# Retention and a softplus feed-forward layer on one core: step 8's scores moved behind step 7's values, and the weights loaded and converted in another order

## The chip, the cores and the metric

The kernel runs on one core of one Trainium2 chip. The metric is the device time of one execution in microseconds (us); the kernel before has a median of 818.29 us over three runs (818.12 to 818.95). A core has five engines with a queue each, which run their own instructions in program order: TensorE (PE, with its weight loads as PEld), VectorE (DVE), ScalarE (ACT), GpSimd (POOL) and SyncE (SP, which issues the DMA transfers here). They wait for each other through semaphores.

## The reference

```python
def _attn_ref(q, k, v):                      # batch 8, heads 8, sequence 576, head width 64
    scores = scale * np.matmul(q, k.transpose(0, 1, 3, 2))
    Dmat = np.where(rel >= 0, gamma[:, None, None] ** rel[None, :, :], 0.0)
    return np.matmul(scores * Dmat[None, :, :, :], v)
def _moe_ref(x, w_in, w_out):                # 4608 tokens, 512 -> 2048 -> 512
    h = x @ w_in
    g = np.maximum(h, 0.0) + np.log1p(np.exp(-np.abs(h)))
    return g @ w_out
```

The attention output, with its heads side by side, is the `x` of the feed-forward layer.

## The kernel before

The attention is computed in its recurrent form, in **steps** of two head pairs by 128 tokens. For each step TensorE makes scores (`scores`, `scores_whole`), sums of keys and values (`sums`), values (`values`), and the products with the state so far ("cross"). VectorE masks the scores into `a` (or `a_whole`), updates the state `s`, and scales the values out into `x`. ScalarE scales the step's `v` in place (`scale_values`; for steps 9 and later GpSimd does it), and writes the high part of `x` into `xt`; the low part (`x` minus the high part) is a subtraction on GpSimd or VectorE. The feed-forward products run as three products of high and low parts.

The 4608 tokens are nine units of 512. The **opening** (`for m in range(AHEAD)`, AHEAD = 9, FIRST = 8) does steps 0 to 7 for unit 0 whole, and begins step 8 for unit 1. Then come 16 **slots** (`for i in range(NF)`): slot i makes `h` for hidden block i of unit 0 (12 matmuls, from first-layer weight `win i`), its softplus, and the 12 output matmuls `y` of the block before (from second-layer weight `wout i-1`). Every odd slot also has the next attention step in front of its `h`. After the slots the tail of the kernel begins with one more attention product group (`chunk_products` of steps 17 and 16), followed by products whose weights come through a ring of buffers (`ring`).

**Weights.** There are 32 weight pieces of 512 KB, piece 2p for `win p` and 2p+1 for `wout p`. They lie in memory in 64 bits, and each is converted while it is used for the first time: `weight_p` (ScalarE, high word), `weight_t` (VectorE, low word), `weight_b` (VectorE, joins them in `wst`), `weight_c` (ScalarE, high part into `win` or `wout`), `weight_d` (VectorE, low part). They stage through the five buffers of `wst`; `weight_dl` does the last part, starts the load of a further piece into a freed buffer, and stores a first-layer piece back to memory in its two parts (`split`). The function `weight_a` is `weight_p` and `weight_t`.

The order on each engine is the order in which the code is written. All loads go through SP's queue: eight semaphores are used in turn, so that a load waits until the load eight places ahead of it has landed, and a wait holds back whatever stands behind it.

When the last weight is through, the pool of `wst` is closed, and its memory goes to the ring and to the buffers named `odd`, one of which takes the `qv` (queries and values) of step 17:

```python
if n + 2 >= NPIECE and "ring" not in later:
    weight_pools.close()
    ...
    load_step(2 * CHUNKS - 1)
    scale_values(2 * CHUNKS - 1)
    for _ in range(RING):
        block_load()
```

Of the kernel before, what the change touches and what calls it, by code (L numbers as in the profile page):

```python
# [27 lines left out]
NF = DF // P  # L28
# [9 lines left out]
NCONST = SMALL + NPAIR * C  # L38
PIECE = 512
FIRST = AHEAD - 1  # L40
START_WEIGHTS = 3
OPENING = 3
NOPEN = AHEAD + 2
CHUNKS = 9
# [39 lines left out]
def retention_softplus_ffn(ctx: ExitStack, tc, first, whole, others, consts, w, out):  # L84
# [73 lines left out]
    def load_step(m):  # L158

        if m == 0:  # L160
            at = 0
            for x in parts:
                nc.sync.dma_start(x, first[:, at:at + x.shape[1]])
                at += x.shape[1]
            k, q = parts[0][:, 0:2 * C], parts[0][:, 2 * C:4 * C]
            kp, v = parts[1][:, 0:2 * C], parts[1][:, 2 * C:4 * C]
        else:
            if m < NOPEN:
                place = openp if m < OPEN1 else openp2
                r = place.tile([P, 8 * C if m < FIRST else RAW], F32, name=f"raw{m}")  # L170
                nc.sync.dma_start(r, whole[m - 1] if m < FIRST else others[m - FIRST])
                keys, qv = r[:, 0:KEYS], r[:, KEYS:]
            else:
                load_keys(m)
                load_rest(m)
                return
            k, kp, q, v = keys[:, 0:2 * C], keys[:, 2 * C:], qv[:, 0:-2 * C], qv[:, -2 * C:]
        live[m] = {n: x.rearrange("p (s c) -> p s c", s=2) for n, x in dict(k=k, q=q, kp=kp, v=v).items()}
# [201 lines left out]
    def state_whole(m, L):  # L380
        before = states.get(m % 2)
        total = L["T"].rearrange("p (s d) -> p s d", s=2)
        whole, at = of_chunk("s", [m], 2), halves_of([m])
        s = whole[:, at]
        if before is None:
            nc.vector.tensor_copy(s, total)
        else:
            nc.vector.tensor_add(s, total, before[:, at])
        f = constant[0][1][:, at]
        nc.gpsimd.tensor_mul(s, s, f.unsqueeze(2).broadcast_to([P, 2, D]))  # L390
        states[m % 2] = whole
# [15 lines left out]
    def values_out(m, rest):  # L407

        L = live.pop(m)
        ch, pr = m // 2, 2 * (m % 2)  # L410
        cols = slice((ch % CPU) * C, (ch % CPU + 1) * C)
        hi, lo = (xt[:, n, T1 + m % 2, :, cols] for n in (HI, LO))
        x = openp.tile([P, 2, C], F32, tag="x", name="x", bufs=2)
        nc.vector.tensor_mul(x, L["O"], constant[0][2][:, pr:pr + 2])

        def parts_out():
            nc.scalar.copy(hi, x)
            rest.tensor_sub(lo, x, hi.bitcast(F32))
        return parts_out
# [129 lines left out]


    wl = {}

    def load_weight(n):
        if n < NPIECE:
            wl[n] = wst.tile([P, PIECE, 2], I32, tag="wst", name="wst", bufs=WBUFS)
            nc.sync.dma_start(wl[n].rearrange("p c a -> p (c a)"), w[n // 2, n % 2])

    def weight_a(n):
        weight_p(n)
        weight_t(n)  # L560
# [14 lines left out]
    def weight_b(n):  # L575
        if n >= NPIECE:
            return
        hi, lo = wl[n][:, :, 1], wl[n][:, :, 0]
        nc.vector.scalar_tensor_tensor(hi, hi, 3, lo, op0=ALU.logical_shift_left, op1=ALU.bitwise_or)
# [9 lines left out]
    def weight_c(n):  # L589
        if n in wl:  # L590
            nc.scalar.copy(weight_dst(n)[0], wl[n][:, :, 1].bitcast(F32))

    def weight_d(n):
        if n in wl:
            head, rest = weight_dst(n)
            nc.vector.tensor_sub(rest, wl.pop(n)[:, :, 1].bitcast(F32), head.bitcast(F32))  # L596

    def weight_store(n):
        if n < NPIECE and n % 2 == 0:
            nc.sync.dma_start(split[n // 2].bitcast(F32), wins[n // 2].bitcast(F32))  # L600

    def weight_dl(n):
        if n in wl:
            weight_d(n)
            load_weight(n + WBUFS)
            weight_store(n)


# [77 lines left out]
            nc.sync.dma_start(to.bitcast(F32), a)  # L686


    first_a, first_b = {3: 0, 5: 1, 6: 2}, {4: 0, 6: 1}
    first_weights = {4: (0,), 6: (1,), 7: (2,), 8: (3,)}  # L690
    fill = moe.tile([P, T], F32, tag="ab", name="fill", bufs=ABUFS)
    nc.vector.memset(fill, 1.0)
    for m in range(AHEAD):
        load_step(m)
        for n in first_weights.get(m, ()):
            load_weight(n)
    load_step(AHEAD)
    nc.sync.dma_start(consts_sb, consts)
    load_weight(WBUFS - 1)
    mask_whole = openp.tile([P, C], F32, name="mask_whole")  # L700
    for x, at in ((mask_whole, [slice(0, P)]), (mask, rows)):
        nc.gpsimd.memset(x, 1.0)
# [9 lines left out]
    def next_scores(m):  # L712
        new = ps_open.tile([P, 2, T], F32, tag="pair", name="pair")
        if m < FIRST:
            scores_whole(m, new)
        else:
            scores(m, new)
        return new
# [4 lines left out]
    for m in range(AHEAD):  # L723
        if m < FIRST:
            bank = (ps_att if m % 2 else ps_val).tile([P, 2, T], F32, tag="bank" if m % 2 else "val", name="bank")
            sums_whole(m, bank)
            values_whole(m, bank)
            if m == 0:
                next_scores(1)
            if m + 2 < AHEAD:  # L730
                new = next_scores(m + 2)
            ready = live[m]
            if m < FIRST - 1:
                state_whole(m, ready)
            if m == 0:
                scale_values(1)
            if m + 2 < AHEAD:
                scale_values(m + 2)
            parts_out = values_out(m, nc.gpsimd if m < FIRST - 1 else nc.vector)
            if m == 0:  # L740
                masked_whole(1)
            if m + 2 < FIRST:
                masked_whole(m + 2)
            if m == FIRST - 1:
                weight_b(2)
            parts_out()
            if m == FIRST - 1:
                weight_c(2)
            if m == FIRST - 1:
                scale_values(AHEAD)  # L750
                state_whole(m, ready)
        else:
            sums(m, new)
            scores_out(m)
            states_out(m)
        if m in first_a:
            weight_a(first_a[m])
        if m in first_b:
            weight_b(first_b[m])
            weight_c(first_b[m])  # L760
        if m == 5:
            weight_dl(0)
        if m == AHEAD - 1:
            weight_d(2)
        if m == AHEAD - 2:
            load_step(AHEAD + 1)
    weight_dl(1)
    load_weight(WBUFS + 2)
    weight_store(2)
    psum_pools.close()  # L770
    first_pools.close()
    later["xs"] = pool("xs", 1).tile([P, 4, 2, T], F32, name="xs")
# [3 lines left out]


    for i in range(NF):
        n = START_WEIGHTS + 2 * i
        m = AHEAD + (i - 1) // 2  # L780
        step = i % 2
        if step:
            bank = ps_att.tile([P, 2, T], F32, tag="bank", name="bank")
            scores(m, bank)
            sums(m, bank)
            values(m - 1, bank)
            if i < NF - 1 and m + 1 >= NOPEN:
                load_step(m + 1)
        weight_p(n)
        weight_t(n)  # L790
        weight_c(n - 1)
        weight_b(n)
        weight_t(n + 1)
        h = hidden_mm(i, i % 2)
        ab = logs(h)
        if i:
            weight_dl(n - 1)
        if i < NF - 1:
            softplus(h, ab)
        if step:  # L800
            _, t, cols = place(m - 1)
            where = (B11, B21)[(m - 1) % 2], STAGE[(m - 1) % 2, t], cols
            halves_out(m - 1)
            scores_out(m)
            states_out(m)
            if i < NF - 1:
                scale_values(m + 1)
            if m == NOPEN:
                open_pools.close()
                place_weights(ctx.enter_context(tc.tile_pool(name="wpool2", bufs=1)), NF)  # L810
        if i == NF - 1:
            softplus(h, ab)
        weight_c(n)
        if not step:
            weight_dl(n)
        gs[0, i] = softplus_split(ab)
        softplus_rest(gs[0, i], ab)
        if step:
            weight_dl(n)
            half_x(*where, nc.gpsimd)  # L820
        weight_p(n + 1)
        weight_b(n + 1)
        if n + 2 >= NPIECE and "ring" not in later:
            weight_pools.close()
            for name, bufs in (("ring", RING), ("odd", 2)):
                later[name] = ctx.enter_context(tc.tile_pool(name=name + "2", bufs=bufs))
# [4 lines that stand above are left out]
        output_some(CPU)  # L831
        outputs_of(0, i)
# [591 lines left out]
```

## Time and profile before

| what | value |
|---|---|
| median of the runs | 818.29 us |
| profiled execution, its own time | 818.9 us |
| its span from first to last instruction | 816.9 us |
| TensorE busy | 808.6 us (99%) |
| VectorE busy | 563.5 us (69%) |
| ScalarE busy | 389.5 us (48%) |
| GpSimd busy | 122.6 us (15%) |
| mean granted clock of TensorE | 0.999 |

The profiled execution is one run, and the sum of the prediction is made against it. Between its span and its own time lie 2.0 us of start and end, and its time is 0.6 us above the median of the runs. The spans of TensorE's matmuls are pipelined, so the time from one start to the next says more than the length of one.

### The profile page before, as it was taken

The numbers are of one execution on the slowest core, as the hardware profiler recorded it, in microseconds if no ns is written. First come the engines' busy times: TensorE is split into PE (matmuls) and PEld (weight loads), VectorE is DVE, ScalarE is ACT, GpSimd is POOL, SyncE is SP. The second block draws the span as 40 slices with busy tenths as digits, with TensorE's granted clock in tenths as the row PEclk, the third lists the DMA queues.
The fourth block names the chain that finished last, engine by engine and source line by source line (L and its number), as shares of the span: only waits on it lengthen the run. The fifth ranks groups of instructions, "written<-read, shape, count | busy, mean of one in ns | idle before, by whom it ended". The sixth has DMA issues, their size and how long they took to land.

```text
span 816.9 us, 18675 instructions
## 1 busy us (share of the span) xinstructions
PE 808.6 (99%) x7319; PEld 666.3 (82%) x7319; DVE 563.5 (69%) x953; ACT 389.5 (48%) x681; POOL 122.6 (15%) x223
## 2 busy tenths in 40 slices
PE   8999999999999999999999999999999999999998
PEld 6788888888888888888888888888888888888886
DVE  5999976777666874867669974555679944335785
ACT  6888773334423244434344554324355734434553
POOL 4323321211311420112112001121100000000000
PEclk9999999999999999999999999999999999999999
DMA  9898969989799882798897777878656786666674
GB/s 364 313 299 301 321 235 386 335 290 346 263 312 361 308 314 80 234 327 274 301 301 232 220 227 242 264 235 260 217 175 217 210 254 195 195 191 195 193 220 160
DMA packets 149847, 211.75 MB, mean 259 GB/s; under 512 B 10880, under 2 KB 114816, under 8 KB 149760
## 3 DMA queue, kind: packets, MB, share of 16 engines
q1 hardware_dynamic: 149760, 210.56, 78.4%
q8 instruction: 59, 0.97, 0.5%
q14 instruction: 28, 0.23, 0.1%
HBM read 168.05 MB, written 42.47 MB: 258 GB/s over the span
## 4 chain that ended last, share of the span: by engine, by line
PE 96%; DMA 3%; DVE 1%; SPq 0%; issue 0%; DVEq 0%
PE acc L876 22%; PE sum L1168 20%; PE y L510 16%; PE two L876 13%; PE h L476 5%; PE two L1168 4%; PE third L876 3%; PE third L210 2%; PE third L1168 2%; PE acc L1168 2%; PE two L194 2%; PE two L298 2%; DMA raw<-others 1%; PE two L310 1%; DMA raw<-whole 1%; DMA wst<-w 1%
## 5 line engine op out<-in xcount | busy, mean ns | idle before, releaser
L876 PE MATMUL acc<-xt,ring 128*128 128x512 f32 x780 | 196.3, 389 | 0.0
L1168 PE MATMUL sum<-parts,ring 128*128 128x512 f32 (+1 forms) x723 | 173.7, 391 | 0.0
L876 PEld LDWEIGHTS acc<-xt,ring 128*128 128x128 f32 x780 | 146.3, 188 | 30.6
L1168 PEld LDWEIGHTS sum<-parts,ring 128*128 128x128 f32 x723 | 134.2, 188 | 28.2
L1161 DVE TENSOR_TENSOR parts<-g,parts 128x512 fp32r<-128x512 f32 x168 | 115.4, 694 | 45.0 <-ACT parts L1157 42.2
L510 PE MATMUL y<-wout,g 128*128 128x512 f32 x576 | 140.1, 392 | 0.7 <-DVE g L498 0.7
L1157 ACT CAST parts<-g 128x512 fp32r<-128x512 f32 x168 | 103.9, 622 | 68.0 <-DVE parts L1161 28.8
L510 PEld LDWEIGHTS y<-wout,g 128*128 128x128 f32 x576 | 107.1, 188 | 23.6 <-PE h L476 1.1
L876 PE MATMUL two<-xt,ring 128*128 128x512 f32 x486 | 123.3, 389 | 0.0
L876 PEld LDWEIGHTS two<-xt,ring 128*128 128x128 f32 x486 | 91.2, 188 | 18.9
L1178 ACT ACTIVATE g<-g 128x512 f32<-128x512 f32 x72 | 45.3, 629 | 60.6 <-DVE g L1193 35.6
L187 POOL TENSOR_TENSOR qv<-qv,consts_sb 128x256 f32<-128x256 f32 x61 | 46.7, 766 | 162.8 <-DMA qv<-others 155.6
L1193 DVE TENSOR_TENSOR g<-two,g 128x512 f32<-128x512 f32 x24 | 16.6, 692 | 77.9 <-PE two L876 77.9
L1191 ACT COPY g<-acc 128x512 f32<-128x512 f32 x24 | 14.1, 586 | 77.6 <-PE acc L876 77.6
L498 DVE TENSOR_TENSOR g<-ab,g 128x512 fp32r<-128x512 f32 x42 | 32.0, 762 | 25.5 <-ACT g L494 24.9
L494 ACT CAST g<-ab 128x512 fp32r<-128x512 f32 x42 | 26.1, 620 | 47.6 <-PE y L510 41.5
L476 PE MATMUL h<-xt,win 128*128 128x512 f32 x192 | 47.5, 396 | 0.3 <-DVE win L596 0.3
L476 PEld LDWEIGHTS h<-xt,win 128*128 128x128 f32 x192 | 35.3, 188 | 8.4 <-DVE win L596 0.8
L1231 ACT ACTIVATE g<-acc 128x512 f32<-128x512 f32 x24 | 14.3, 598 | 48.1 <-PE acc L876 48.1
L210 PEld LDWEIGHTS third<-qv,keys 64*64 64x64 f32 x776 | 27.0, 134 | 8.9 <-issue 8.5
L252 DVE TENSOR_TENSOR a<-two,mask 128x512 f32<-128x512 f32 (+1 forms) x28 | 19.0, 678 | 21.9 <-PE third L210 15.0
L1168 PE MATMUL two<-parts,ring 128*128 128x512 f32 x144 | 33.6, 389 | 0.0
(173 smaller groups left out, 1183.8 us busy)
## 6 DMA issues: line engine op xcount, KB each, us to landing
ring<-split SPq DMA_DIRECT2D x121, 256.0 KB, 4.5
ring<-combined SPq DMA_DIRECT2D x108, 256.0 KB, 3.8
ring<-outcombined SPq DMA_DIRECT2D x96, 256.0 KB, 3.5
qv<-others SPq DMA_DIRECT2D x61, 320.0 KB, 5.4
ring<-outsplit SPq DMA_DIRECT2D x72, 256.0 KB, 3.6
wst<-w SPq DMA_DIRECT2D x32, 512.0 KB, 6.0
keys<-others SPq DMA_DIRECT2D x61, 256.0 KB, 5.4
split<-win SPq DMA_DIRECT2D x16, 512.0 KB, 6.3
```

What stands on the lines that cost most here:

```text
L187: nc.gpsimd.tensor_mul(v, v, f.unsqueeze(2).broadcast_to([P, 4, D]))
L210: mm = nc.tensor.matmul(L["T"][rows[h], t, part[s]], L["kp"][rows[t], s, rows[h]], L["v"][rows[t], s, rows[h]], start=True, stop=True, ski ...
L252: nc.vector.tensor_mul(a[:, :, at], src.rearrange("p h (s c) -> p h s c", c=HC), mask.unsqueeze(1).unsqueeze(1).broadcast_to([P, 2, 2 * le ...
L476: nc.tensor.matmul(h, wins[p][:, a, kt * P:(kt + 1) * P], xt[:, b, T1 + half, kt % 2], start=(n == 0), stop=(n == 3 * NKT - 1))
L494: nc.scalar.copy(g[:, HI], ab)
L498: nc.vector.tensor_sub(g[:, LO], ab, g[:, HI].bitcast(F32))
L510: nc.tensor.matmul(ys[u][tt], g[:, a, tt * P:(tt + 1) * P], wouts[p][:, b], start=(p == 0 and n == 0), stop=(p == NF - 1 and n == 2))
L876: nc.tensor.matmul(bank, w[:, ta, kt * P:(kt + 1) * P], xt[:, tb, x, kt], start=start and k == 0, stop=k == 5, skip_group_check=True)
L1157: nc.scalar.copy(t[:, HI], g_slot(J, n))
L1161: nc.vector.tensor_sub(t[:, LO], g_slot(J, n), t[:, HI].bitcast(F32))
L1168: nc.tensor.matmul(bank[m][:, x], w[:, a, m * P:(m + 1) * P], t[:, b, x], start=start and n == 0, stop=n == 2, skip_group_check=True)
L1178: nc.scalar.activation(c, c, AF.Softplus)
```

## The change

Three things are changed together, all in the opening and the 16 slots.

- Step 8's scores are issued behind step 7's values on TensorE, not ahead of step 7's sums. The low part of step 7's `x` is made by GpSimd, not by VectorE.
- The pieces are loaded in the order 0, 2, 1, 4, 3, 6, 5, ... (`weight_order`), which puts `win p+1` ahead of `wout p`, and the second piece stands behind the load of step 7's inputs, not ahead of it.
- `win 1` is converted in the opening in place of `wout 0` and `win 1`; `wout i` is converted in slot i, where before it was `wout i+1`. So the last piece, `wout 15`, is converted at the end of slot 14, behind everything else of that slot. In slot 1 the results of the attention are taken (`attention_out`) behind the softplus, not ahead of it.

```diff
+    weight_order = [0] + [n for p in range(1, NF) for n in (2 * p, 2 * p - 1)] + [NPIECE - 1]
...
     def weight_dl(n):
         if n in wl:
             weight_d(n)
-            load_weight(n + WBUFS)
+            if weight_order:
+                load_weight(weight_order.pop(0))
             weight_store(n)
...
     for m in range(AHEAD):
         load_step(m)
-        for n in first_weights.get(m, ()):
-            load_weight(n)
+        if m in (FIRST // 2, FIRST - 1, FIRST):
+            load_weight(weight_order.pop(0))
     load_step(AHEAD)
+    load_weight(weight_order.pop(0))
     nc.sync.dma_start(consts_sb, consts)
-    load_weight(WBUFS - 1)
+    load_weight(weight_order.pop(0))
...
-            if m + 2 < AHEAD:
-                new = next_scores(m + 2)
+            if m + 2 < FIRST:
+                next_scores(m + 2)
             ready = live[m]
             if m < FIRST - 1:
                 state_whole(m, ready)
+            else:
+                new = next_scores(FIRST)
...
-            parts_out = values_out(m, nc.gpsimd if m < FIRST - 1 else nc.vector)
+            parts_out = values_out(m, nc.gpsimd)
...
     for i in range(NF):
-        n = START_WEIGHTS + 2 * i
+        n, win = 2 * i + 1, 2 * i + 2
...
-        weight_p(n)
-        weight_t(n)
-        weight_c(n - 1)
-        weight_b(n)
-        weight_t(n + 1)
+        if i == 2:
+            weight_c(win)
+            weight_dl(win)
+        if i < NF - 1:
+            weight_a(n)
+        weight_c(win)
+        if i < NF - 1:
+            weight_b(n)
+        weight_dl(win)
+        if i > 1:
+            weight_t(win + 2)
         h = hidden_mm(i, i % 2)
         ab = logs(h)
-        if i:
-            weight_dl(n - 1)
+        if i == 1:
+            weight_t(win + 2)
...
+        if i == NF - 2:
+            weight_a(n + 2)
+            weight_b(n + 2)
+            weight_c(n + 2)
+            weight_dl(n + 2)
+        if i == NF - 2 and "ring" not in later:
             weight_pools.close()
```

How this moves the instructions is shown at three places. First TensorE at the end of the opening, before (`raw6` to `raw9` are the inputs of steps 6 to 9, `pair` is the bank of step 8's scores, `h` is the first hidden block):

```order
L376 MATMUL bank_470<-raw6_203 64x64 x4
L398 MATMUL bank_470<-a_whole_423,raw6_203 64x128 x4
L403 MATMUL bank_470<-raw6_203,s_414 64x128 x4
L194 MATMUL pair_483<-raw8_211 64x64 x8
L376 MATMUL bank_507<-raw7_207 64x64 x4
L398 MATMUL bank_507<-a_whole_460,raw7_207 64x128 x4
L403 MATMUL bank_507<-raw7_207,s_414 64x128 x4
L210 MATMUL pair_483<-raw8_211 64x64 x4
L476 MATMUL h_568<-xt_186,win0_428 128x512 x12
```

The same place in the change:

```order
L375 MATMUL bank_468<-raw6_203 64x64 x4
L397 MATMUL bank_468<-a_whole_423,raw6_203 64x128 x4
L402 MATMUL bank_468<-raw6_203,s_414 64x128 x4
L375 MATMUL bank_496<-raw7_205 64x64 x4
L397 MATMUL bank_496<-a_whole_460,raw7_205 64x128 x4
L402 MATMUL bank_496<-raw7_205,s_414 64x128 x4
L193 MATMUL pair_509<-raw8_209 64x64 x8
L209 MATMUL pair_509<-raw8_209 64x64 x4
L475 MATMUL h_560<-xt_186,win0_428 128x512 x12
```

The eight matmuls of step 8's scores have gone behind the three groups of step 7, and nothing else moved on TensorE in the whole program. Second, SP's queue of loads in the opening, before (`wst` is a weight piece; by the code the pieces are 0, 1, 2 and 3):

```order
L556 DMA wst_199<-w 128x1024
L171 DMA raw5_201<-whole 128x1024
L171 DMA raw6_203<-whole 128x1024
L556 DMA wst_205<-w 128x1024
L171 DMA raw7_207<-whole 128x1024
L556 DMA wst_209<-w 128x1024
L171 DMA raw8_211<-others 128x1152
L556 DMA wst_213<-w 128x1024
L171 DMA raw9_215<-others 128x1152
```

And in the change, where the pieces are 0, 2, 1 and 4:

```order
L556 DMA wst_199<-w 128x1024
L170 DMA raw5_201<-whole 128x1024
L170 DMA raw6_203<-whole 128x1024
L170 DMA raw7_205<-whole 128x1024
L556 DMA wst_207<-w 128x1024
L170 DMA raw8_209<-others 128x1152
L556 DMA wst_211<-w 128x1024
L170 DMA raw9_213<-others 128x1152
L556 DMA wst_215<-w 128x1024
```

The inputs of steps 7, 8 and 9 each have one piece less ahead of them. Third, VectorE from slot 14's weights to slot 15's attention results (`xs`), before; `ab` is the softplus, `g` its low part, and L596 is `weight_d`:

```order
L573 TENSOR_SCALAR wst_1451<-wst_1451 128x512
L579 SCALAR_TENSOR_TENSOR wst_1451<-wst_1451 128x512
L596 TENSOR_TENSOR win15_1568<-wst_1409,win15_1568 128x512
L490 SCALAR_TENSOR_TENSOR ab_1584<-h_1571,ab_1584 128x512
L596 TENSOR_TENSOR wout15_960<-wst_1451,wout15_960 128x512
L498 TENSOR_TENSOR g_1593<-ab_1584,g_1593 128x512
L437 TENSOR_TENSOR xs_557<-bank_1636,consts_sb_105 128x2x128
```

And in the change:

```order
L573 TENSOR_SCALAR wst_1426<-wst_1426 128x512
L579 SCALAR_TENSOR_TENSOR wst_1426<-wst_1426 128x512
L596 TENSOR_TENSOR win15_1563<-wst_1402,win15_1563 128x512
L489 SCALAR_TENSOR_TENSOR ab_1581<-h_1568,ab_1581 128x512
L596 TENSOR_TENSOR wout14_952<-wst_1426,wout14_952 128x512
L497 TENSOR_TENSOR g_1588<-ab_1581,g_1588 128x512
L573 TENSOR_SCALAR wst_1450<-wst_1450 128x512
L579 SCALAR_TENSOR_TENSOR wst_1450<-wst_1450 128x512
L596 TENSOR_TENSOR wout15_953<-wst_1450,wout15_953 128x512
L436 TENSOR_TENSOR xs_544<-bank_1636,consts_sb_105 128x2x128
```

The last piece's three instructions, the end of which frees `wst`, stand behind `g` of slot 14, where before they stood ahead of it.

## Rows read from the trace of the kernel before

**Rows 1.** All waits of TensorE in the whole span: us in total, times, longest us

```profile
PE idle L710 <- DVE fill L692: 1.5, 1, 1.5
PE pair L361 <- DMA raw<-whole: 1.4, 3, 0.5
PE y L510 <- DVE g L498: 0.7, 1, 0.7
PE pair L194 <- DMA raw<-others: 0.6, 1, 0.6
PE h L476 <- DVE win L596: 0.3, 1, 0.3
```

**Rows 2.** Timeline, 0 to 26 us: start us, us, engine, line, operation [idle before]

```profile
11.99 0.33 SPq L171 DMA_DIRECT2D raw<-others  x1
13.27 0.33 SPq L698 DMA_DIRECT2D consts_sb<-consts  x1
...
18.51 0.67 PE L361 MATMUL pair<-raw 64*64 64x128 f32 x16 [0.34 <-DMA raw<-whole]
...
21.21 0.46 PE L194 MATMUL pair<-raw 64*64 64x64 f32 x16 [0.63 <-DMA raw<-others]
...
23.24 3.01 PE L476 MATMUL h<-xt,win 128*128 128x512 f32 x12
...
24.14 0.83 DVE L418 TENSOR_TENSOR xt<-x,xt 128x256 fp32r<-128x256 f32 x1
```

**Rows 3.** Timeline of slots 0 to 3, from logs to output matmuls

```profile
27.58 0.63 ACT L486 ACTIVATE ab<-ab 128x512 f32<-128x512 f32 x1
...
28.59 0.68 DVE L490 SCALAR_TENSOR_TENSOR ab<-h,ab 128x512 f32<-128x512 f32 x1
...
29.96 0.69 DVE L498 TENSOR_TENSOR g<-ab,g 128x512 fp32r<-128x512 f32 x1
...
30.80 2.97 PE L510 MATMUL y<-wout,g 128*128 128x512 f32 x12 [0.67 <-DVE g L498]
...
33.97 0.68 DVE L490 SCALAR_TENSOR_TENSOR ab<-h,ab 128x512 f32<-128x512 f32 x1
...
43.07 0.42 DVE L573 TENSOR_SCALAR wst<-wst 128x512 int32<-128x512 uint32 x1
...
43.93 0.60 ACT L484 ACTIVATE ab<-h 128x512 f32<-128x512 f32 x1
...
47.75 0.68 DVE L498 TENSOR_TENSOR g<-ab,g 128x512 fp32r<-128x512 f32 x1
```

**Rows 4.** Chain that ended last, slots 3 and 5: start us, us

```profile
49.33 2.72 PE y L510 x12
...
61.53 2.72 PE y L510 x12
```

**Rows 5.** Timeline of ScalarE, slots 7 and 9

```profile
68.33 0.60 ACT L484 ACTIVATE ab<-h 128x512 f32<-128x512 f32 x1
...
79.83 0.67 ACT L591 CAST win<-wst 128x512 fp32r<-128x512 f32 x1 [0.21 <-DVE wst L579]
80.53 0.60 ACT L484 ACTIVATE ab<-h 128x512 f32<-128x512 f32 x1
```

**Rows 6.** Timeline at the changeover from the slots to the tail

```profile
112.18 0.69 DVE L579 SCALAR_TENSOR_TENSOR wst<-wst 128x512 int32<-128x512 int32 x1
...
114.34 0.68 DVE L596 TENSOR_TENSOR wout<-wst,wout 128x512 fp32r<-128x512 f32 x1
...
115.05 0.33 SPq L152 DMA_DIRECT2D qv<-others  x1
115.12 0.69 DVE L498 TENSOR_TENSOR g<-ab,g 128x512 fp32r<-128x512 f32 x1
...
118.45 0.61 POOL L187 TENSOR_TENSOR qv<-qv,consts_sb 128x256 f32<-128x256 f32 x1 [6.67 <-issue]
...
119.88 0.24 PE L210 MATMUL third<-qv,keys 64*64 64x64 f32 x1
```

**Rows 7.** DMA issues by size over the whole span: KB each, median us to landing

```profile
out<-quad SPq DMA_DIRECT2D x2, 128.0 KB, 1.9
```

More of the change, by code (lines that the diff above doesn't have):

```diff
@@ L40 @@
 FIRST = AHEAD - 1
-START_WEIGHTS = 3
 OPENING = 3
@@ L686, in combine_store @@
             nc.sync.dma_start(to.bitcast(F32), a)
-    first_a, first_b = {3: 0, 5: 1, 6: 2}, {4: 0, 6: 1}
-    first_weights = {4: (0,), 6: (1,), 7: (2,), 8: (3,)}
     fill = moe.tile([P, T], F32, tag="ab", name="fill", bufs=ABUFS)
@@ L743, in retention_softplus_ffn @@
                 masked_whole(m + 2)
-            if m == FIRST - 1:
-                weight_b(2)
             parts_out()
[L747 to L751, printed above, removed]
         else:
@@ L755, in retention_softplus_ffn @@
             states_out(m)
[L756 to L761, printed above, removed]
+        if m == FIRST - 5:
+            weight_a(0)
+        if m == FIRST - 4:
+            weight_b(0)
+            weight_c(0)
+        if m == FIRST - 3:
             weight_dl(0)
-        if m == AHEAD - 1:
-            weight_d(2)
-        if m == AHEAD - 2:
+        if m == FIRST - 2:
             load_step(AHEAD + 1)
-    weight_dl(1)
-    load_weight(WBUFS + 2)
-    weight_store(2)
+            weight_a(2)
+        if m == FIRST - 1:
+            weight_b(2)
+            scale_values(AHEAD)
+            state_whole(m, ready)
     psum_pools.close()
@@ L788, in retention_softplus_ffn, with attention_out @@
                 load_step(m + 1)
-        weight_p(n)
-        weight_t(n)
-        weight_c(n - 1)
-        weight_b(n)
-        weight_t(n + 1)
+        if i == 2:
[9 more added lines that the diff above has]
+            weight_t(win + 2)
         h = hidden_mm(i, i % 2)
         ab = logs(h)
-        if i:
-            weight_dl(n - 1)
+        if i == 1:
+            weight_t(win + 2)
         if i < NF - 1:
             softplus(h, ab)
-        if step:
-            _, t, cols = place(m - 1)
-            where = (B11, B21)[(m - 1) % 2], STAGE[(m - 1) % 2, t], cols
+        def attention_out():
             halves_out(m - 1)
@@ L810, in retention_softplus_ffn @@
                 place_weights(ctx.enter_context(tc.tile_pool(name="wpool2", bufs=1)), NF)
+        if step:
+            _, t, cols = place(m - 1)
+            where = (B11, B21)[(m - 1) % 2], STAGE[(m - 1) % 2, t], cols
+            if i > 1:
+                attention_out()
         if i == NF - 1:
@@ L816, in retention_softplus_ffn @@
         gs[0, i] = softplus_split(ab)
+        if i == 1:
+            weight_p(win + 2)
         softplus_rest(gs[0, i], ab)
+        if i == 0:
+            weight_t(win + 2)
         if step:
             weight_dl(n)
+        if i == 1:
+            weight_b(win + 2)
+            attention_out()
+        if step:
             half_x(*where, nc.gpsimd)
-        weight_p(n + 1)
-        weight_b(n + 1)
-        if n + 2 >= NPIECE and "ring" not in later:
+        if i != 1:
+            weight_p(win + 2)
+            weight_b(win + 2)
+        if i == NF - 2:
[4 more added lines that the diff above has]
+        if i == NF - 2 and "ring" not in later:
             weight_pools.close()
```

## Prediction

> **What bounds the kernel now.** I began with the list of all waits of TensorE [rows 1]. It is short: the five rows are all there is, 4.5 us in a span of 816.9, and the last of them (0.3, for `win 2`) ends at 34 us. From there to the end TensorE, the bound of the kernel, waits for no one. So the change can win only what TensorE waits for in the opening and in the first three slots, and it loses whatever new wait it makes. I then read the timeline of the opening [rows 2]: the scores of steps 7 and 8 each wait for their inputs (0.34 and 0.63), and slot 0's `h` starts at 23.24. Third, the timeline of the first slots [rows 3], where `y` waits 0.67 for the softplus. Fourth, the loop of VectorE and ScalarE through the slots against TensorE's own period [rows 4, 5]. Last, the changeover to the tail [rows 6], where TensorE begins step 17's sums at 119.88.
>
> **Opening: about 1.1 us won.** Two loads that follow each other land 1.28 us apart: SP's two issues at 11.99 and 13.27 each waited for one landing of 512 KB [rows 2]. In the new order the inputs of steps 7 and 8 have one piece less ahead of them, so they come 1.28 earlier, more than either waits. Both waits go: 0.34 + 0.63 = 0.97. Step 8's scores also no longer hold up step 7's sums; that is worth a little more, and I put `h` at 22.1, 1.1 earlier (bounds 0.6, if one of the waits stays in part, and 1.35). Step 7's low part moves from VectorE (0.83, [rows 2]) to GpSimd; only the 11th matmul of `h`, some 2.3 us after the first (12 take 2.72, [rows 4]), reads it, which covers it twice over. Without that cover it would cost its 0.8.
>
> **Slots 0 to 3: 1.4 us won in all.** From `h`'s start to the first `y` it takes 30.80 − 23.24 = 7.56 us [rows 2, 3]. In it VectorE comes late to the softplus: the logs end at 28.21, and it starts at 28.59. In the change VectorE has less ahead of it (two conversions in the opening, not three), so 0.38 goes too: `y` at 22.1 + 7.56 − 0.38 = 29.3, which is 1.5 earlier. The wait for `win 2` goes, since its piece is converted by then. But VectorE itself doesn't stay 1.5 ahead. Behind `g` of slot 0 one more conversion of a low word (0.42, [rows 3]) now stands ahead of what `win 2` needs, so slot 1's softplus is about 1.2 ahead of its 33.97. And in slot 1 the attention results, which before filled VectorE's time while ScalarE made the high part of `g`, stand behind it: the same instructions follow, plus about 0.75 of waiting (the length of a softplus or `g`, as in rows 3, plus handing over). So VectorE and ScalarE reach slot 3 only some 0.5 to 0.85 ahead of where they were; I take 0.7, against the start of slot 3's logs at 43.93.
>
> TensorE can't run away from them, because each `y` needs its `g`. In slot 3 `g` ends at 48.43 and `y` starts at 49.33 [rows 3, 4]; handing over takes 0.15 (30.65 to 30.80, [rows 3]), so 0.75 is slack. TensorE's gain at slot 3 is then 0.7 + 0.75 = 1.45 at most, about what it brought. The rest comes back as a wait of `y` for `g` of a few tenths.
>
> From slot 3 to 13 TensorE keeps its period of 12.20 for two slots (61.53 − 49.33, [rows 4]). VectorE and ScalarE are a little quicker if left alone: logs at 68.33, and the conversion ahead of the next odd slot's logs ends by 80.50, where they start at 80.53, just as `h` ends [rows 5]. With the overlap of a tenth that such rows have, their period is 12.05 to 12.17. They catch up 0.03 to 0.15 in each of five rounds, and are 0.85 to 1.45 ahead in slot 14. I take 1.4, nearer to the end that TensorE's own lead sets.
>
> **Changeover: all of it lost again.** This is the term that decides. The load of step 17's `qv` goes into memory that `wst` held: before, `wout 15`'s last instruction ends at 115.02, and SP issues the load at 115.05 [rows 6]. In the change three VectorE instructions and a ScalarE one follow `g` of slot 14 in a chain: `g` 115.12 + 0.69, low word 0.42 [rows 3], joining 0.69, high part on ScalarE 0.67 [rows 5], low part 0.68 [rows 6], together 118.27, say 118.2 with overlaps. The chain is 3.2 us later; less VectorE's lead of 1.4, it ends at 116.8. Behind the load stand, in this order, GpSimd's scaling of step 17's values and TensorE's first sums, and behind the load on SP's queue the eight loads of the ring.
>
> How long the load takes can be bounded. Before, GpSimd started 3.40 after the issue, with step 17's keys queued ahead of it (118.45, [rows 6]). On an empty queue a transfer of 128 KB took 1.9 [rows 7]; 192 KB more at 1.28 for 512 adds 0.5, so 2.4. I take 2.9: the queue will be empty, but no row shows this size alone. The Trainium skill, "DMA: Bandwidth & Descriptors", section "Anatomy of one DMA — SWDGE (gpsimd) path", gives a fixed 2.0 us and the bytes at 436 GB/s; for 320 KB that is an estimate of 2.75, by which the sum would be 0.15 lower. No run here shows it.
>
> So: issue 116.85, scaling from 119.75 to 120.36 (0.61), TensorE at 120.43, against 119.88. The second half of the group needs two small GpSimd copies that queue behind the scaling, 0.1 more. Without the wait TensorE would be there at 119.88 − 1.45 = 118.4; it stands idle for 2 us. From here on nothing differs: TensorE had no wait after this point, and the ring's loads shift along with it.
>
> **Sum.** 120.43 + 0.1 − 119.88 = +0.65 us on the profiled execution's 818.9; on the median, which is 0.6 below that, **818.9**. Its bounds: a lead of 2.1 (nothing limits it: 1.1 + 0.67 + 0.34) with 2.4 for the load gives −0.55; a lead of 0.7 with 3.4 gives +1.85.
>
> **The rivals.**
> *The gain stays.* If the load at the changeover were covered (its buffer free before `wout 15` is done, or the chain shorter than I add it up), the 1.45 to 1.65 of the first slots remain: 816.7. For it: before, TensorE doesn't wait at the changeover [rows 1]. Against it: the issue three hundredths after `wout 15`'s end, and no slack behind it (scaling ends at 119.06, use at 119.88: 0.8 us to give for 3.2 less the lead). Chance 0.1.
> *Slower by VectorE's lag.* If VectorE and ScalarE bring no lead into slot 14, because they lose in slots 1 and 2 what they won or because their new order has a longer period than 12.20, then the changeover costs its full price: with a lead of 0.5 and 3.2 for the load, +1.9, so 820.2; with TensorE waiting for `g` in every odd slot besides, up to 821. It decides as soon as the lead in slot 14 is under 0.7. For it: the two periods differ by 0.15 at most [rows 4, 5], so a lead once lost comes back slowly. Against it: from slot 3 on both orders have the same instructions for two slots. Chance 0.17.
> *It does nothing.* If step 7's inputs are not what the opening waits for (the next wait, for the scaling of step 8's values, takes over), `h` wins under 0.3, and the lead stays small, the changeover still asks its price and the case before applies; only with a short load (2.4) do gain and loss cancel, at 818.3. Chance 0.08.
>
> **How the numbers follow.** The forecast (a gain of 1.45 that the changeover more than takes back, 817.7 to 820.1) has 0.65. About 0.2%, or 1.64 us, is what a measurement of this kernel can tell from no change: faster means under 816.65, slower over 819.93. The faster rival at 816.7 lies half on either side of that bound: 0.06 faster. Slower takes most of its rival and the top edge of the forecast: 0.17. The rest, 0.77, is the same. The range goes from 817.2, inside the gap between forecast and the faster rival, to 820.3, which takes in the middle of the slower one.
>
> **What the profile would show.** Right: slot 0's `h` near 22.1; no DMA wait of steps 7 and 8 among TensorE's waits; the first `y` near 29.3; `y` of slot 5 about 1.4 before its 61.53; one new wait of about 2 us of TensorE for step 17's `qv` (DMA or GpSimd) between 118 and 121; the load issued right behind `wout 15`'s low part, near 116.8. Wrong in the first step, if `h` starts after 22.6; in the second, if `y` waits for `g` in many slots; in the third, if TensorE starts step 17's sums before 119. The whole would be wrong if a transfer in the tail, which now starts later, came too late for a matmul after 121.

## The result, and the profile after

The change takes 823.2 us (median of four runs, 821.8 to 824.21) against 818.62 for the kernel before: a ratio of 1.0055, with a 95% interval from 1.0037 to 1.0072. That is slower, and above the range of 817.2 to 820.3. Six more runs of the same kernel gave 822.09 (820.91 to 823.95), ratio 1.0049 [1.0037, 1.0060]. The profiled execution took 824.21, with a span of 822.2 against 816.9 before, so 5.3 us have to be found.

First all waits of TensorE in the profile of the change, in the columns of [rows 1]:

```profile
PE third L209 <- POOL qv L186: 2.0, 1, 2.0
PE idle L710 <- DVE fill L691: 1.5, 1, 1.5
PE y L509 <- issue: 1.4, 1, 1.4
PE y L509 <- DVE wout L596: 0.6, 2, 0.4
PE y L509 <- DVE g L497: 0.3, 1, 0.3
PE pair L360 <- DMA raw<-whole: 0.2, 1, 0.2
```

The waits of the opening for steps 7 and 8 are gone, as forecast. New are the wait of 2.0 for step 17's `qv`, also forecast, two waits of `y` for `wout`, and one of 1.4 behind which the profile shows nothing ("issue"). Next the timeline of TensorE through the opening and the first slots, and of VectorE in slot 3:

```profile
21.49 3.02 PE L475 MATMUL h<-xt,win 128*128 128x512 f32 x12
...
28.72 3.00 PE L509 MATMUL y<-wout,g 128*128 128x512 f32 x12
...
42.21 3.02 PE L509 MATMUL y<-wout,g 128*128 128x512 f32 x12 [0.32 <-DVE g L497]
...
47.19 0.68 DVE L497 TENSOR_TENSOR g<-ab,g 128x512 fp32r<-128x512 f32 x1
47.79 0.89 DVE L596 TENSOR_TENSOR wout<-wst,wout 128x512 fp32r<-128x512 f32 x1
47.93 0.50 PE L509 MATMUL y<-wout,g 128*128 128x512 f32 x1
48.83 2.76 PE L509 MATMUL y<-wout,g 128*128 128x512 f32 x11 [0.40 <-DVE wout L596]
```

Slot 0's `h` starts 1.75 earlier than before (23.24, [rows 2]) and the first `y` 2.08 earlier (30.80, [rows 3]). In slot 3 little of that is left: the first matmul of `y` runs at 47.93, and the second has to wait until VectorE has made the low part of `wout 3` right behind `g`. In slot 5, `y` starts at 61.06, 0.47 ahead of [rows 4].

Part of these distances is not the change's. In the profile of the kernel before, step 6's scores waited 0.53 for their input, whose load stands at the same place in both orders, and slot 3's `y` started at 49.17:

```profile
16.09 0.67 PE L361 MATMUL pair<-raw 64*64 64x128 f32 x16 [0.53 <-DMA raw<-whole]
...
49.17 2.88 PE L510 MATMUL y<-wout,g 128*128 128x512 f32 x12
```

The kernel of a later experiment ("The last piece late") has the same opening and the same slots up to the 13th, and its profile is without that wait:

```profile
22.58 3.02 PE L476 MATMUL h<-xt,win 128*128 128x512 f32 x12
...
48.22 2.88 PE L510 MATMUL y<-wout,g 128*128 128x512 f32 x12
```

Against this one the change's `h` starts 1.09 earlier, but the second matmul of its `y` in slot 3 starts 0.4 later (48.83 against 48.45): none of the gain is left there.

The changeover, in the timeline (compare [rows 6]):

```profile
114.35 0.69 DVE L497 TENSOR_TENSOR g<-ab,g 128x512 fp32r<-128x512 f32 x1
114.96 0.42 DVE L573 TENSOR_SCALAR wst<-wst 128x512 int32<-128x512 uint32 x1
115.48 0.69 DVE L579 SCALAR_TENSOR_TENSOR wst<-wst 128x512 int32<-128x512 int32 x1
116.21 0.65 ACT L591 CAST wout<-wst 128x512 fp32r<-128x512 f32 x1 [1.32 <-DVE wst L579]
...
116.89 0.69 DVE L596 TENSOR_TENSOR wout<-wst,wout 128x512 fp32r<-128x512 f32 x1 [0.71 <-ACT wout L591]
...
117.61 0.33 SPq L151 DMA_DIRECT2D qv<-others  x1
...
120.83 0.61 POOL L186 TENSOR_TENSOR qv<-qv,consts_sb 128x256 f32<-128x256 f32 x1 [9.07 <-DVE g L497]
121.49 0.27 PE L209 MATMUL third<-qv,keys 64*64 64x64 f32 x1 [2.02 <-POOL qv L186]
...
122.81 4.60 PE L896 MATMUL acc<-xt,ring 128*128 128x512 f32 x12
```

The last row is one group of twelve matmuls. Such a group takes 3.0 in the rows above, and 4.60 here. The next view, the windows of TensorE behind the wait (length, busy time with the count of instructions, granted clock, DMA share, GB/s), says why:

```profile
120.00:122.00 2.00, 0.51 (x32) 1.00 0.90 262
122.00:124.00 2.00, 2.00 (x41) 0.76 0.81 241
124.00:126.00 2.00, 2.00 (x6) 0.50 0.98 316
126.00:128.00 2.00, 2.00 (x9) 0.89 1.05 385
128.00:130.00 2.00, 2.00 (x11) 1.00 1.02 407
```

Right behind the wait the granted clock falls to 0.50, the level of 1.2 GHz, and is back at 1.00 by 128 us. The wait marked "issue" stands further on, in the middle of a `y`:

```profile
168.56 2.35 PE L509 MATMUL y<-wout,g 128*128 128x512 f32 x9 [1.40 <-issue]
```

Matching TensorE's instructions of both profiles in order shows where the distance grows: step 17's sums are 1.61 later than before, the first ring product 1.85, the next `y` 3.40 (127.24 against 123.84), the product after the "issue" wait 5.10 (170.75 against 165.65), and the end 5.3.

### The profile page after: what moved, and what is told of

Same layout as the page of the kernel before. It is cut to its first block, busy times and chain, and to the rows that moved or that the text cites. A ratio compares the mean times of both kernels' runs of the same rounds, so it can differ in the third digit from the quotient of the medians.

```text
span 822.2 us, 18681 instructions
## 1 busy us (share of the span) xinstructions
PE 812.3 (99%) x7319; PEld 667.6 (81%) x7319; DVE 563.8 (69%) x952; ACT 389.3 (47%) x681; POOL 122.7 (15%) x224
## 4 chain that ended last, share of the span: by engine, by line
PE 91%; DVE 2%; ACT 1%; issue 0%; POOL 0%; DVEq 0%
PE acc L896 22%; PE sum L1188 20%; PE y L509 14%; PE two L896 13%; PE two L1188 4%; PE h L475 3%; PE third L896 3%; PE third L209 2%; PE third L1188 2%; PE acc L1188 2%; PE two L193 2%; PE two L297 2%; PE two L309 1%; DVE ab L489 0%; DVE g L497 0%; DVE wst L579 0%
## 5 line engine op out<-in xcount | busy, mean ns | idle before, releaser
L209 PE MATMUL third<-qv,keys 64*64 64x64 f32 x776 | 32.8, 222 | 2.0 <-POOL qv L186 2.0
```

The source lines that it names most:

```text
L209: mm = nc.tensor.matmul(L["T"][rows[h], t, part[s]], L["kp"][rows[t], s, rows[h]], L["v"][rows[t], s, rows[h]], start=True, stop=True, ski ...
```

## The experiments

Theory A: the time is lost where the load of step 17's `qv` waits for `wout 15`, and in what follows that wait; the opening's gain was spent before, because `y` waits for `wout i`. Rival B: the new order of conversions slows the slots themselves. Rival C: the ring's loads, which also come later, are what costs.

**The last piece ahead again.** In slot 14 the change's own lines are moved ahead of the softplus and `g`:

```diff
+        if i == NF - 2:
+            weight_a(n + 2)
+            weight_b(n + 2)
         h = hidden_mm(i, i % 2)
...
         weight_c(n)
+        if i == NF - 2:
+            weight_c(n + 2)
         if not step:
             weight_dl(n)
+        if i == NF - 2:
+            weight_dl(n + 2)
         gs[0, i] = softplus_split(ab)
...
-        if i == NF - 2:
-            weight_a(n + 2)
-            weight_b(n + 2)
-            weight_c(n + 2)
-            weight_dl(n + 2)
```

> The change, with one thing put back: the last weight piece (`wout 15`) is converted ahead of slot 14's `h` and of its `g`, as in the kernel before. Theory A (the time was lost where step 17's `qv` is loaded late behind `wout 15`, and in what follows from that wait): the load is issued about 2.5 us earlier, near 115, TensorE doesn't wait for step 17, its granted clock stays at 1.00 between 120 and 130 us, and the small lead of the slots (about 0.4 us) is kept: 818.0 to 818.6. Rival B (the loss lies in the slots, where VectorE now has to convert `wout i` in the same slot): the changeover matters little, 821 to 823 as the change has.

Measured: 819.98, ratio to the kernel before 1.0018 [1.0010, 1.0026]. About two thirds of the loss is gone, so B falls as the main cause; but the time is 1.4 above what A gave. The clock is 1.00 from 120 to 130 us. The load was issued at 115.88, not near 115, and the timeline shows two short waits in place of the long one:

```profile
119.80 0.27 PE L209 MATMUL third<-qv,keys 64*64 64x64 f32 x1 [0.28 <-POOL qv L186]
...
120.11 0.69 DVE L497 TENSOR_TENSOR g<-ab,g 128x512 fp32r<-128x512 f32 x1 [0.68 <-ACT g L493]
...
120.15 0.81 POOL L279 COPY sx<-u 64x128 f32<-64x128 f32 x1
...
121.02 0.27 PE L309 MATMUL two<-qv,sx 64*64 64x64 f32 x1 [0.42 <-POOL sx L279]
```

GpSimd's copy took 0.81 where the same copy took 0.29 in the change (121.85). It ran beside VectorE's `g`, and came as late as it did because the scaling ahead of it waits for the load.

**The last piece late, in the kernel before.** The kernel before, with piece 31 left out of its slot's conversions (`if n < NPIECE - 1`) and this behind the rest of slot 14:

```diff
+        if n == NPIECE - 1:
+            weight_a(n)
+            weight_b(n)
+            weight_c(n)
+            weight_dl(n)
```

> The kernel before, with one thing of the change: the conversion of the last piece (`wout 15`) stands behind everything else of slot 14. Theory A: the load of step 17's `qv` is issued about 3.2 us later than 115.05 and TensorE waits 2.0 to 2.7 us at step 17; if its granted clock then falls as in the change, 1.5 us more: 821 to 823; if the clock holds, about 821. Rival B (the slots' order is what costs): 818.6, no new wait.

Measured: 821.97 (820.9 to 822.99), ratio 1.0038 [1.0026, 1.0051], as A gave. This edit alone makes most of the slowdown (the change's ratios are 1.0055 and 1.0049): the load is issued at 117.43, TensorE waits 2.46, and the clock falls in the profiled execution. From step 17's sums to the `y` behind them the distance to the kernel before grows by 1.57 (1.43 to 3.00), against 0.24 (1.75 to 1.99) in a profile of the change in which the clock held (below); so the low clock cost 1.3 here. Its step 17 and its windows:

```profile
121.31 0.27 PE L210 MATMUL third<-qv,keys 64*64 64x64 f32 x1 [2.46 <-POOL qv L187]
```

```profile
120.00:122.00 2.00, 0.69 (x33) 0.91 0.84 225
122.00:124.00 2.00, 2.00 (x34) 0.50 0.92 304
124.00:126.00 2.00, 2.00 (x8) 0.73 0.99 321
```

**A buffer of its own for step 17.** The change, with one condition of `load_rest` altered, so that `qv` of step 17 goes where the earlier inputs went, and only the ring waits for `wst`:

```diff
-        place = later["odd"] if m >= 2 * CHUNKS - 1 and m % 2 else rawp
+        place = later["odd"] if m >= 2 * CHUNKS + 1 and m % 2 else rawp
```

> The change, with step 17's `qv` loaded into the buffers of the attention inputs, not into memory that `wst` held; the ring stays in `wst`'s memory. So the load of `qv` no longer has to wait for `wout 15`, and only the ring's first weights do. Theory A: the wait for `qv` goes, and a shorter one (up to 1.0 us) may come at the first matmul that uses the ring; the clock holds or falls less: 818.2 to 819.5. Rival C (the ring's late loads are what costs): the wait of about 2 us moves to the ring, 821 to 823. Rival B (the slots): 821 to 823 without a wait at the changeover.

Measured: 819.11, ratio 1.0004 [0.9994, 1.0013]: the change's loss is gone. Three rows of its timeline:

```profile
49.21 2.77 PE L509 MATMUL y<-wout,g 128*128 128x512 f32 x11 [0.41 <-DVE wout L596]
...
114.57 0.39 SPq L151 DMA_DIRECT2D qv<-others  x1
...
119.93 0.24 PE L209 MATMUL third<-qv,keys 64*64 64x64 f32 x1
```

The load goes out 3.0 us earlier than in the change, and TensorE starts step 17 without a wait. The ring's loads went out earlier as well here (from 115.01, in the change from 118.00), so this run alone doesn't tell C from A; against C stands that in the change's profile no matmul waits for a ring load. What also shows is that the opening's gain does not reach the end: from the wait of 0.41 in slot 3 on, TensorE stands within 0.2 of its times in the profile of the kernel before.

**The wait filled.** Matmuls that only add work, on data that lie ready, into a bank that step 17 overwrites; nine, and in a second kernel four (of 512 columns, 0.23 us each, in both; the 128 of the first expectation is wrong):

```diff
+            for _ in range(9):
+                nc.tensor.matmul(later["two"][:, 0], xt[:, HI, T1, 0, 0:P], xt[:, HI, T1, 0], start=True, stop=True, ...)
```

> The change, with nine more matmuls of 128 columns on TensorE just ahead of step 17's scores; their results are overwritten, so they only add work in the time in which TensorE waits for `qv`. They take 1 to 2 us of a wait of 2.0. Theory A with the clock as a cost of its own: TensorE still begins step 17's sums at about 121.5, but the granted clock stays at 1.00 in 122 to 130 us, so the 1.5 us behind the wait are saved: 821.3 to 821.8. Rival (the slow stretch isn't due to the wait, or the wait alone is the loss): the clock falls as before and the time is that of the change, about 823, or more where the added matmuls push step 17 back.

> The change, with four more matmuls of 512 columns in the wait for step 17's `qv` (results overwritten). They take 0.9 us, so that TensorE still stands still for about 1.1 us, and step 17 isn't pushed back. If it is the length of the wait that brings the clock down: granted clock 1.00 from 122 to 130 us and about 1.4 us less than the change. If any wait there does it: the clock falls as in the change and the time is that of the change.

Measured: 823.54 (ratio 1.0066 [1.0050, 1.0083]) with nine, 822.17 (1.0050 [1.0038, 1.0062]) with four. Behind the wait the clock held in both profiles, but the times were not better. With nine, the windows show:

```profile
120.00:122.00 2.00, 2.00 (x25) 1.00 0.95 261
122.00:124.00 2.00, 2.00 (x57) 1.00 0.86 270
124.00:126.00 2.00, 2.00 (x10) 1.00 1.03 338
```

The `y` behind step 17 starts at 125.90, 1.34 before that of the change. But the filled kernel loses it again further on, above all at a stop of 1.0 at `two` (L309), whose releaser the profile doesn't show either. With four, TensorE stands still for 1.20 at step 17, and the profile has its low clock elsewhere, in the opening:

```profile
10.00:12.00 2.00, 2.00 (x28) 0.50 1.03 422
```

Two of these eleven runs show a mean granted clock of 0.998 or less, against ten of 16 with the wait left open (ten runs of the change, six with the late last piece), and one of the two is this profile. So the fall goes with the standstill. That its 1.5 us are simply added to the time, these two kernels do not show: the four runs of the second at 0.999 or more still took 821.6 to 822.8.

**The change again.**

> The change itself once more, for a median of more runs on the same chip as the others. Theory A: TensorE's wait of about 2.0 us at step 17 and the stretch of granted clock at half come again, the 1.4 us wait in the middle of a `y` (which nothing that the profile shows ended) does not come at the same place: 821.5 to 823. If that wait belongs to the change it comes again at about 167 us, and the median is 823 to 824.

Measured: 822.09. In its profiled execution (820.91, span 818.9) TensorE waited 2.10 at step 17, until GpSimd's scaling (120.96 to 121.57), but the clock held and no "issue" wait came. The profile puts this wait down to a load of the ring; but the matmul reads only `qv` and the keys, and starts 0.06 behind the scaling, as in the first profile (0.05). The clock:

```profile
122.00:124.00 2.00, 2.00 (x53) 1.00 0.99 311
124.00:126.00 2.00, 2.00 (x10) 1.00 1.05 345
126.00:128.00 2.00, 2.00 (x10) 1.00 1.08 400
```

Step 17's products with the state are 1.93 later than before, and so is all that follows: span +2.0. So the wait came in both profiles of the change, the clock's fall in one. Of ten runs of the change, six show a mean granted clock of 0.998 or less; their median is 823.6, that of the other four 821.4. Of the six runs of the kernel before with the late last piece, four do. Such a mean does not say where the clock fell, as the profile with four matmuls shows; but without a wait over 1 us it is rare: one of 12 with the last piece ahead, none of 12 with the own buffer, two of 67 runs of the kernel before in the same series (of the kernels below, the opening alone had three of 12 in one series and none of 11 in the next, the other two none of 11 and two of 11).

**Opening alone.** The kernel before with the opening's order of scores and loads, and nothing of the new conversions:

```diff
-    first_weights = {4: (0,), 6: (1,), 7: (2,), 8: (3,)}
+    first_weights = {4: (0,), 7: (1,), 8: (2,)}
...
+    load_weight(3)
...
-            if m + 2 < AHEAD:
-                new = next_scores(m + 2)
+            if m + 2 < FIRST:
+                next_scores(m + 2)
...
+            else:
+                new = next_scores(FIRST)
```

> The kernel before, with the opening of the change alone: step 8's scores behind step 7's values, and the inputs of steps 7, 8 and 9 each loaded one weight piece earlier; the pieces keep their order and all conversions their places. If the opening's gain survives where `wout i` is converted a slot ahead (theory A: the change lost its gain because `y` of slots 1 to 3 waits for VectorE, which converts `wout i` in the same slot): `h` of slot 0 about 1 us earlier than 23.24, TensorE still about 1 us ahead of 49.33 at slot 3, no wait at step 17 over 0.3: 817.4 to 817.9. Rival: VectorE can't keep that lead in the old order either, and `y` waits for `g`: 818.3 to 818.8, no change.

> The opening alone once more, since a quarter of its runs showed a lower clock. If the gain is real: most runs 817.2 to 818.0, below those of the kernel before by 0.7 or more; if it was the luck of the first runs: 818.0 to 818.6.

Measured: 817.75, and again 817.82, where the kernel before had 818.49 and 818.38. The medians are 0.74 and 0.56 lower; the ratios, 1.0001 [0.9989, 1.0012] and 0.9994 [0.9985, 1.0002], don't exclude no change. The first series had three of 12 runs at a lower clock (820.4 to 821.2), the second none of 11. In the first profile `y` of slot 3 starts as one group, 1.40 before the 49.17 at which the same timeline of before shows it, and step 17 starts 1.41 earlier, without a wait:

```profile
47.77 2.88 PE L510 MATMUL y<-wout,g 128*128 128x512 f32 x12
...
117.34 0.62 POOL L187 TENSOR_TENSOR qv<-qv,consts_sb 128x256 f32<-128x256 f32 x1 [6.95 <-issue]
118.47 0.24 PE L210 MATMUL third<-qv,keys 64*64 64x64 f32 x1
```

In the second profile step 6's scores wait 0.53, as in the kernel before; slot 3's `y` starts at 48.22, and TensorE ends 0.73 ahead. But 48.22 is also where the run with the late last piece had it, whose opening is the old one. So a gain of about 0.6 is likely by the medians and not shown beyond the noise. What the profiles do show is that a lead at slot 3 lasts where `wout i` is converted a slot ahead, and that the conversions' new order takes it away: there the second matmul of slot 3's `y` starts at 48.83 to 49.21 in five profiles, with `h` at 21.48 to 21.86; here at 47.99 and 48.45, with `h` at 21.71 and 22.25.

**State updates behind `wout`.** The own buffer, and in slots 3 to 13 `states_out` and `scale_values` moved behind `g` and `wout i`:

```diff
             scores_out(m)
+            if i == 1 or i == NF - 1:
+                attention_rest()
+        def attention_rest():
             states_out(m)
...
         if step:
             weight_dl(n)
+        if step and 1 < i < NF - 1:
+            attention_rest()
```

> The change with step 17's `qv` in a buffer of its own (as in the earlier run), and in slots 3 to 13 the attention's state updates moved behind the softplus and `wout i` on VectorE. Theory A (what holds TensorE back in slots 1 to 3 is VectorE's work ahead of `wout i`): the `y` of slot 3 comes 0.5 to 1.2 us earlier than in the run with the buffer alone, and most of that reaches the end: 818.0 to 818.6. Rival (slots 1 and 2 have spent the lead already, at their waits for `g`): `y` of slot 3 gains no more than its own wait of 0.4: 818.7 to 819.1.

Measured: 818.89, ratio 1.0005 [0.9996, 1.0013]. The first part of A's forecast came: `y` of slot 3 starts as one group at 47.53, where with the buffer alone its second matmul stood at 49.21, and behind it TensorE is 1.3 ahead of that run, though its `h` was only 0.66 ahead. So VectorE's work ahead of `wout i` was what held it. But it did not reach the end. TensorE is still 1.03 ahead at 200 us, and at 282 it waits for a mark that GpSimd sets behind other work:

```profile
281.24 0.90 POOL L458 TENSOR_TENSOR quad<-xs,quad 128x256 f32<-128x256 f32 x1
282.09 0.09 POOL L347 MEMSET mark<- 1x1 f32 x1
...
282.24 0.68 PE L209 MATMUL third<-qv,keys 64*64 64x64 f32 x16 [0.87 <-POOL mark L347]
```

**Opening with the low part on GpSimd.** The opening alone, with `values_out(m, nc.gpsimd)` for step 7 too, as in the change:

> The kernel before with the opening of the change and, of the change, also the low part of step 7's `x` on GpSimd; weights as in the kernel before. With the opening alone the first `y` waited 0.9 for `g`, because VectorE reached the softplus 0.6 after the logs. Without the low part's 0.66 on VectorE that wait falls to about 0.3, and as nothing in slots 1 to 3 took the lead back there: 817.0 to 817.3 where the clock holds. Rival: VectorE's other work in slots 0 to 3 takes the place of the low part, as in the change, and the time is that of the opening alone, 817.4 to 817.7.

Measured: 817.79, ratio 0.9993 [0.9984, 1.0002], no better than the opening alone. The wait of the first `y` for `g` fell from 0.9 to 0.2, but a new one stands ahead of it:

```profile
25.62 0.63 POOL L273 COPY sx<-s 64x128 f32<-64x128 f32 x1
...
26.31 0.27 PE L310 MATMUL bank<-raw,sx 64*64 64x64 f32 x1 [0.40 <-POOL sx L273]
```

The low part now lies in GpSimd's queue ahead of this copy, and step 8's products wait for it. The prediction's sentence that the move is covered twice over looked at `h` alone.

## Why the prediction was wrong, point by point

**Opening: right in the mechanism; what it brought beyond the forecast is luck.** `h` at 21.49 (forecast 22.1, bounds 21.9 to 22.6), both waits gone. The first `y` came at 28.72, where 29.3 was forecast. Of the 1.75 at `h`, 1.1 was forecast, and 1.09 is the distance to the profile in which step 6's scores did not wait; most of the rest lies in the 0.53 that the profile of the kernel before happened to lose there.

**Slots 0 to 3: the step that failed first.** "TensorE's gain at slot 3 is then 0.7 + 0.75 = 1.45 at most, about what it brought": the limit was taken from `g` alone. But the change also puts `wout i` into the slot whose `y` uses it, behind `g` on VectorE; that conversion, 0.89 in slot 3, stands in the way of the second matmul of `y`. The 0.75 of slack behind `g` was thus spent, and TensorE kept 0.47. The opening alone, where `wout i` stays a slot ahead, keeps 1.40 in the same place (0.95 in its second profile), and moving VectorE's state updates behind `wout i` brings 1.3 back.

**Changeover: the right mechanism, two terms mis-sized.** The chain from slot 14's `g` to the end of `wout 15` takes 114.35 to 117.58, 3.23, where 3.08 was forecast (115.12 to 118.2). The lead that was set against it is 0.77 (`g` at 114.35 against 115.12, [rows 6]) instead of 1.4, which the step before explains: it was put "nearer to the end that TensorE's own lead sets", and that lead was 0.47. The load takes 3.22 from issue to scaling instead of 2.9: it landed 2.91 after its issue, and the 0.31 from there to the scaling is missing in the lower bound of 2.4, since [rows 7] counts to the landing. The issue is 0.76 late against the forecast (117.61 against 116.85), the load 0.32, and 0.02 comes back in handing over: step 17 at 121.49, not 120.43. The copies behind it cost 0.24, not 0.1. The estimate of 2.75 by the Trainium skill ("DMA: Bandwidth & Descriptors", section "Anatomy of one DMA — SWDGE (gpsimd) path") comes from a fit for DMAs that GpSimd issues. This load, issued through SP on an empty queue, took 3.21 to 3.29 to the scaling in five profiled executions with the late piece, so the estimate was further off than the row.

**"From here on nothing differs": failed, and in the profiled execution this is the larger part.** Behind the wait the clock cost 1.55 (3.40 − 1.85), the "issue" wait with what lies around it 1.70 (5.10 − 3.40), and small stops some 0.2. With the forecast's +0.65, the 1.06 and 0.14 of the changeover and these 3.45, the sum is 5.3, the measured difference of the profiled executions. With the lead, the load and the copies put right the sum would be +1.85, or 820.1 on the median, still inside the range; what lies behind the wait carried the time out of it. The clock is not all of that: the four runs of the change without a low clock have a median of 821.4, and only the fastest of them, 820.91, is profiled. The sum was made as if a TensorE that stands still for 2 us went on at the speed it had before.

**The rivals.** "Slower by VectorE's lag" was nearest: its "lead of 0.5 and 3.2 for the load, +1.9" is what an execution with the clock at 1.00 shows (+1.93 behind step 17). It was given 0.17 because "from slot 3 on both orders have the same instructions for two slots", which counts instructions and leaves out which of them `y` waits for. Even it ended at 821, since no case held the clock's part. For the "issue" wait no cause was found: it came in one of two profiled executions of the change and none of the kernel before, and no run here tells whether it belongs to the change.

## What to carry to other kernels

When a conversion is moved closer to its use, look for the use's second operand: here `y` needs `g` and `wout`, and a slack that was read behind one of them was gone because the other now ended last. When a change leaves the bound engine standing, add a term for what its clock does behind the standstill, and give it a chance of its own, since it comes in some executions only. And a gain early in a long kernel has to pass every later place that is tied to another engine: one step's load, one mark in a queue can take it back.

## What the runs showed of the hardware that was not expected

- After TensorE stood still for 2.0 to 2.5 us, having run at 1.00 for over 100 us, its granted clock fell to 0.50 in the two profiled executions shown above and held in a third, with the same wait. Low mean clocks in six of ten and four of six runs fit this, though a mean does not say where the clock fell. With the wait filled by matmuls, or 0.9 us of it filled, the clock held there, in one profile each. That a busy or idle TensorE sets the level is what the Trainium skill states ("TensorE: Matmul & The Clock Gate", section "Part 1: The HAM clock gate (the "warmup" mystery)"); these traces agree, and add that one wait of this length may or may not bring it down.
- A copy on GpSimd took 0.81 beside a VectorE subtraction of two buffers, and 0.29 alone. The Trainium skill ("SBUF — State Buffer", section "SBUF: two separate sides") says that a VectorE instruction with two inputs from SBUF and a GpSimd instruction that reads SBUF block each other; the one case here agrees.
